# Gate logits in a score tile, the gate's exp behind the scores' exps, and a reordered start, in a fused attention and mixture-of-experts kernel

## The chip, the cores and the metric

The kernel runs on one core of one Trainium2 chip. The metric is device microseconds of one execution; the median of several runs is compared. A core has five engines that each work through their own list of instructions in order and wait for each other by semaphores: TensorE (PE; its weight loads are shown apart as PEld), VectorE (DVE), ScalarE (ACT), GpSimd (POOL) and SyncE (SP). Transfers are issued from the lists of POOL, SP and ACT and run on 16 DMA engines that the core's queues share.

## The reference

Sliding-window causal attention for 8 batches, 8 heads, 576 positions and head width 64, then a mixture of experts in which each batch as a whole goes to one expert:

```
scores = scale * q @ k.T                      # masked to 0 <= i - j < 64
attn   = softmax(scores);  x = attn @ v       # [B, S, H*D] = [8, 576, 512]
logits = x.mean(axis=1) @ w_gate              # [B, 8]
e      = argmax(logits, axis=1)
gate_w = softmax(logits)[e]
out[b] = gate_w[b] * (relu(x[b] @ w1[e]) @ w2[e])    # w1: 512 x 1024, w2: 1024 x 512
```

All inputs and the output are float32.

## The kernel before, in words

The work is cut into 16 units (`NU`), two for each batch (four heads each). For a unit the kernel loads q and k as bf16 (`load_qk`), transposes them on TensorE (`transpose_qk`: 18 transposes each, then one copy to SBUF, `leave_qk`; q's copy is ACT's, k's mostly VectorE's), computes the scores in three chunks (`scores`: 14 matmuls, one exp on ACT and, except for units 0 and 1, one mask product on VectorE), the products with v (`values`, twice 20 matmuls into `op`, then a reciprocal and a product on VectorE that give `x`), and the transposes of x (`transpose_x`: 10 transposes, two copies on ACT that also sum, and VectorE's `gate_parts`). v is loaded once for a batch (`load_v`, a DMA on SP's queue that is started behind a small write on POOL) and cast into two f16 layouts `va` and `vb` (`cast_part`: "whole" fills va, "low" and "high" fill the two halves of vb, from va on VectorE or from the f32 tile on POOL).

When both units of a batch are through, `gate(b)` multiplies the parts by ones (tile `gl`, 8 columns), and VectorE takes the largest logit (`gmx`, MAX8), its index (`graw`, FIND_INDEX8), the clamped index (`eidx`) and the bias (`gnm`); POOL loads the index into a register and issues the loads of the chosen expert's w1 and w2. `gate_weight(b)` is the gate's own exp on ACT (`gex`) and a reciprocal on VectorE (`gatew`). The expert's work comes in 13 chunks for a batch: eight up products (`expert_up`: 8 matmuls into `php`, relu on ACT into `hT`) and five down products (`expert_down`, numbered mt = 0, 1, 2, 4, 3; 8 or 16 matmuls into `pso`, a copy `ob` on VectorE, a DMA to the output).

The order on each engine is the order in which the program is written: nothing reorders it. A start part is written out by hand up to unit 3. Then a loop over t = 4 .. 19 works on unit t and calls `experts(pace)` between its pieces; each call puts out expert chunks, from a stream of all batches, until their summed weight reaches the pace. The gate of batch t/2 - 1 stands inside step t when t is even, between the second and the third chunk of scores (for t = 4 between the first and the second). `busy(n)` puts out n matmuls of a constant on TensorE, whose result nobody reads.

All PSUM tiles (scores, `op`, transposes, `gl`, `php`, `pso`, the constants' products) come from one pool of four buffers of 128 x 2 x 512 float32 that are handed out in turn (two banks each): a new tile waits until the last reader of the tile four places before it is done. A score tile uses columns 0 to 383 of each of its two halves.

At the end `row_check` (three VectorE operations over all row sums) and `row_flag` make a flag; if it fails, a general version runs. It does not run here.

Of the kernel before, what the change touches and what calls it, by code (L numbers as in the profile page):

```python
# [9 lines left out]
FP32 = mybir.dt.float32  # L10
# [146 lines left out]
def kernel(  # L157
# [22 lines left out]
    def P(ins):  # L180
        tc.keep_in_program_order(ins)
        return ins
# [169 lines left out]
            copy_on(eng, dst.rearrange("p (x r t) -> p x r t", x=2, t=NT), view)  # L352
            kt_tiles[u] = dst

    sp_ps = {}

    def add_outside(u, c):

        sp = psum.tile([128, 2, 512], FP32, tag="ps", name="sp")
# [4 lines left out]
        sp_ps[u, c] = sp  # L364

    def scores(u, c):
        qT, kT = qt_tiles[u], kt_tiles[u]
        masked = (u, c) in sp_ps
        if not masked:
            sp_ps[u, c] = psum.tile([128, 2, 512], FP32, tag="ps", name="sp")  # L370
        sp = sp_ps[u, c]

        def mm(s, half, kblk, qblk, n):
            P(nc.tensor.matmul(  # L374
                out=sp[64 * half:64 * half + 64, s,
                       64 * (qblk - 6 * c):64 * (qblk - 6 * c) + n],
                lhsT=kT[64 * s:64 * s + 64, ts(kblk, 64)],
                rhs=qT[64 * s:64 * s + 64, 64 * qblk:64 * qblk + n],
                start=not masked, stop=not masked or kblk >= g0 + 4,
                tile_position=(64 * s, 64 * half)))  # L380
# [8 lines left out]
        P(nc.scalar.activation(out=pt, in_=sp[:, :, 0:384], func=AF.Exp, scale=scale))  # L389
        if not masked:  # L390
            P(nc.vector.tensor_tensor(  # L391
                out=pt, in0=pt, in1=masks[:, c].rearrange("p s g w -> p s (g w)"),
                op=ALU.mult))
        pt_tiles[u, c] = pt
# [88 lines left out]

    gate_in = {}

    def gate(b, both=True):
        gl = psum.tile([128, 2, 512], FP32, tag="ps")
        P(nc.tensor.matmul(out=gl[:, 0, 0:E], lhsT=onesf, rhs=gparts[b],
                           start=True, stop=True))
        glog = gl[:, 0, 0:E]  # L490
        gmx = small.tile([128, 8], FP32, tag="gmx")
        P(nc.vector.max(out=gmx, in_=glog))
        graw = small.tile([128, 8], U32, tag="graw")
        P(nc.vector.max_index(out=graw, in_max=gmx, in_values=glog))
# [3 lines left out]
        P(nc.vector.tensor_scalar(out=gnm, in0=gmx[:, 0:1], scalar1=-1.0 / S,  # L498
                                  scalar2=None, op0=ALU.mult))
        gate_in[b] = gl, gnm  # L500
        if both:
            gate_weight(b)

        ereg = nc.gpsimd.alloc_register(f"er{b}")
        P(nc.gpsimd.load(ereg, eidx[0:1, b, 0:1]))
        experts_of[b] = ds(nc.gpsimd.snap(ereg, donate=True), 1)
        weights[b] = (wpool.tile([128, KB, F], FP16, tag="w1t", name=f"w1t{b}"),
                      wpool.tile([128, FB, Dm], FP16, tag="w2t", name=f"w2t{b}"))

    def gate_weight(b):  # L510
        gl, gnm = gate_in[b]
        glog = gl[:, 0, 0:E]
        gex = small.tile([128, E], FP32, tag="gex")
        gsum = small.tile([128, 1], FP32, tag="gsum")
        P(nc.scalar.activation(out=gex, in_=glog, func=AF.Exp, bias=gnm,
                               scale=1.0 / S, accum_out=gsum))
        P(nc.vector.reciprocal(out=gatew[:, b:b + 1], in_=gsum))  # L517
# [48 lines left out]
    def expert_down(b, mt):  # L566
        w2t, hT = weights[b][1], h_tiles[b]
        pso = psum.tile([128, 2, 512], FP32, tag="ps")
        ob = opool.tile([128, Dm], FP32, tag="ob")
        if mt < 4:  # L570
            for fb in range(FB):
                P(nc.tensor.matmul(  # L572
                    out=pso[:, 0, :], lhsT=hT[:, fb, ts(mt, 128)],
                    rhs=w2t[:, fb, :], start=(fb == 0), stop=(fb == FB - 1)))
            P(nc.vector.tensor_copy(out=ob, in_=pso[:, 0, :]))  # L575
            P(nc.sync.dma_start(out=out[b, ts(mt, 128), :], in_=ob))
        else:

            for fb in range(FB):
                for hf in range(2):  # L580
                    P(nc.tensor.matmul(  # L581
                        out=pso[64 * hf:64 * hf + 64, 0, 0:256],
                        lhsT=hT[:, fb, 512:576],
                        rhs=w2t[:, fb, ts(hf, 256)],
                        start=(fb == 0), stop=(fb == FB - 1),
                        tile_position=(0, 64 * hf)))
            P(nc.vector.tensor_copy(out=ob[:, 0:256], in_=pso[:, 0, 0:256]))
# [30 lines left out]
    def expert_chunks():  # L618
        for b in range(B):
            for ft in range(FB):  # L620
                yield (lambda b=b, ft=ft: expert_up(b, ft)), 1.0
            for mt in (0, 1, 2, 4, 3):
                yield (lambda b=b, mt=mt: expert_down(b, mt)), (1.7 if mt < 4 else 0.9)

    stream = expert_chunks()
    acc = [0.0]

    def experts(amount):

        acc[0] += amount  # L630
        while acc[0] > 0.0:
# [3 lines left out]
            nxt[0]()  # L635
            acc[0] -= nxt[1]

    per_step = (8 * 1.0 + 4 * 1.7 + 0.9) / 2
    START = 3

    def busy(n):

        sp = psum.tile([128, 2, 512], FP32, tag="ps", name="idle")
        for _ in range(n):
            P(nc.tensor.matmul(out=sp[:, 0, :], lhsT=spin[:, 0:128], rhs=spin,
                               start=True, stop=True))


    pool0 = {}
# [35 lines left out]
    for c in range(3):  # L685
        scores(0, c)
    make_masks()
    transpose_qk(1, 0)
    transpose_qk(1, 1)
    cast_part(0, "high", nc.gpsimd)  # L690
    cast_part(0, "low", nc.gpsimd)
    load_qk(3)
    load_qk(4)
    cast_part(0, "whole")
    cast_v(1)
    for c in range(3):
        add_outside(1, c)
    for c in range(3):
# [25 lines left out]
    transpose_x(1, eng=V, parts=False)  # L724
    transpose_qk(3, 0)
# [15 lines left out]
    experts(1.0)  # L741
    transpose_x(2)
    values(3, 1)
    experts(1.0)
    transpose_qk(4, 0)
    transpose_qk(4, 1)
    experts(1.0)
    transpose_x(3)

    for t in range(START + 1, NU + LAG):  # L750
        pace = per_step / 8.0 * 0.96
        on, prev, ahead = t < NU, START + 1 < t <= NU, t + 1 < NU

        def next_gate():
            b = t // 2 - 1
            gate(b)
# [92 lines left out]
```

## Time and profile before

| | |
|---|---|
| runs of before | 233.86, 234.08, 235.32 us; median 234.08 |
| profiled execution | 234.69 us, of which the profile's span is 233.0 us |
| TensorE busy / granted clock | 205.6 us (88%) / 0.981 |
| VectorE, ACT, POOL busy | 140.1 us (60%), 122.5 us (53%), 41.2 us (18%) |
| DMA | 45.64 MB, 196 GB/s on average |
| first expert product / last expert product ends | 33.06 us / 225.8 us |

A row of the page or of the timeline gives the start and the length of an instruction or a group in us, the engine, the line of the kernel, the operation, the tile written and those read, and the shape. What stands in brackets is the time that the engine was idle just before, and what ended that idle time. In a view by windows the columns are the stretch, its length, busy time and (in brackets) number of instructions of an engine, the clock granted to TensorE as a share of full speed, the share of the DMA engines' time, and GB/s. In the chain of waits each row is a piece of the work that ended last: start, length, engine, tile, line.

### The profile page before, as it was taken

Reading aid. Unit: us, or ns where it says so; the run is one execution under the profiler, and the core shown is the slowest. Engines: PE = TensorE matmul, PEld = TensorE weight load, DVE = VectorE, ACT = ScalarE, POOL = GpSimd, SP = SyncE. Lnnn points to the kernel's source line nnn. Section 1 sums busy time; section 2 is a strip of 40 time slices with the busy share of each in tenths; the row PEclk is TensorE's granted clock in tenths of the full one; section 3 lists DMA queues with packets and bytes.
Section 4 is the critical chain, followed back from the end, with each engine's and each line's share of the span. In section 5 each row is a group of like instructions: output and inputs, shape, how many; then the busy total and the mean of one; then the engine's idle time right before and its main releaser. Section 6 shows DMA issues by size and latency. Waiting matters only on the chain.

```text
span 233.0 us, 6978 instructions
## 1 busy us (share of the span) xinstructions
PE 205.6 (88%) x3012; PEld 142.2 (61%) x3012; DVE 140.1 (60%) x314; ACT 122.5 (53%) x206; POOL 41.2 (18%) x69
## 2 busy tenths in 40 slices
PE   7656889999799899989999899999998999979970
PEld 2335767745587557855686457856686568639630
DVE  2639596578757777478656777467766672440140
ACT  2344686851668338670957356853677247406300
POOL 7146260055000330025000700020002000200000
PEclk9999599999999999999999999999999999999998
DMA  5999899999999999989999799989911993299231
GB/s 62 242 255 234 134 183 219 246 248 224 230 236 262 263 201 245 231 242 173 238 228 299 132 226 234 251 211 220 258 56 11 204 240 114 26 225 245 89 130 67
DMA packets 29910, 45.64 MB, mean 196 GB/s; under 512 B 2480, under 2 KB 21936, under 8 KB 29872
## 3 DMA queue, kind: packets, MB, share of 16 engines
q0 software_dynamic: 13840, 26.22, 62.8%
q1 hardware_dynamic: 15232, 18.88, 26.9%
q8 instruction: 25, 0.41, 0.7%
q10 hardware_dynamic: 800, 0.03, 0.2%
q14 instruction: 13, 0.11, 0.1%
HBM read 61.90 MB, written 9.44 MB: 306 GB/s over the span
## 4 chain that ended last, share of the span: by engine, by line
PE 50%; DMA 17%; ACT 14%; DVE 13%; issue 3%; POOL 1%; POOLq 0%; ACTq 0%
PE php L558 22%; DMA w1t<-in_moe_w_dram 13%; PE pso L572 13%; ACT xT L458 4%; DMA kn<-in_k_dram 4%; ACT pt L389 4%; PE tp L334 4%; PE op L413 4%; ACT hT L562 3%; PE tp L450 3%; DVE x L429 2%; DVE pt L391 2%; PE sp L374 2%; PE pso L581 2%; DVE dst L303 2%
## 5 line engine op out<-in xcount | busy, mean ns | idle before, releaser
L558 PE MATMUL php<-xT,w1t 128*128 128x288 f16 x512 | 71.6, 288 | 3.3 <-DMA w1t<-in_moe_w_dram 2.2
L562 ACT ACTIVATE hT<-php,gatew 128x576 f16<-128x576 f32 x64 | 47.5, 747 | 32.0 <-PE php L558 31.5
L572 PE MATMUL pso<-w2t,hT 128*128 128x512 f16 x256 | 60.2, 380 | 1.9 <-DVE ob L575 0.8
L558 PEld LDWEIGHTS <-w1t 128*128 128x128 f16 x512 | 54.6, 115 | 10.4 <-DMA w1t<-in_moe_w_dram 3.0
L389 ACT ACTIVATE pt<-sp 128x768 f16<-128x768 f32 x48 | 37.7, 814 | 10.0 <-PE sp L374 10.0
L572 PEld LDWEIGHTS <-hT 128*128 128x128 f16 x256 | 23.1, 98 | 27.6 <-issue 2.4
L575 DVE COPY ob<-pso 128x512 f32<-128x512 f32 x32 | 22.0, 688 | 23.5 <-PE pso L572 23.4
L458 ACT ACTIVATE xT<-tp 128x576 f16<-128x576 f16 x28 | 17.9, 647 | 32.6 <-PE tp L450 32.6
L535 POOL DMA_DIRECT2D w1t<-in_moe_w_dram x7 | 5.0, 717 | 143.8 <-DVE gatew L517 102.7
L391 DVE TENSOR_TENSOR pt<-pt,masks 128x768 f16<-128x768 f16 x42 | 23.3, 555 | 9.8 <-ACT pt L389 9.1
L429 DVE TENSOR_TENSOR x<-op,linv 128x640 f16<-128x640 f32 x32 | 26.4, 825 | 1.1
L303 DVE COPY dst<-tp 128x1152 bf16<-128x1152 bf16 x14 | 19.0, 1356 | 8.7 <-PE tp L334 8.6
L347 ACT COPY dst<-tp 128x1152 bf16<-128x1152 bf16 x16 | 17.9, 1122 | 9.0 <-PE tp L334 9.0
L413 PE MATMUL op<-vb,pt 128*64 128x65 f16 x320 | 16.8, 196 | 4.5 <-DVE pt L391 1.4
L413 PEld LDWEIGHTS <-pt 128*64 128x64 f16 x640 | 13.5, 110 | 11.0 <-issue 6.2
L374 PE MATMUL sp<-dst 64*64 64x128 bf16 (+1 forms) x672 | 16.0, 219 | 2.8 <-DVE dst L303 1.1
L374 PEld LDWEIGHTS <-dst 64*64 64x64 bf16 x672 | 10.9, 110 | 9.8 <-issue 5.0
L413 PE MATMUL op<-va,pt 128*64 128x65 f16 x320 | 16.5, 197 | 0.0
L480 DVE SCALAR_TENSOR_TENSOR gpart<-wg,pooled,gpart 128x8 f32<-128x8 f32 x21 | 4.8, 227 | 18.5 <-ACT xT L458 18.4
L303 DVE COPY vb<-va 64x1152 f16<-64x1152 f16 (+1 forms) x30 | 13.9, 464 | 0.6
L450 PE MATMUL tp<-identh,x 128*128 128x128 f16 x160 | 12.6, 231 | 1.5 <-DVE x L429 1.1
L450 PEld LDWEIGHTS <-x 128*128 128x128 f16 x160 | 10.7, 104 | 4.2 <-DVE x L429 2.9
(70 smaller groups left out, 165.5 us busy)
## 6 DMA issues: line engine op xcount, KB each, us to landing
w2t<-in_moe_w_dram POOLq DMA_DIRECT2D x8, 1024.0 KB, 16.4
out_dram<-ob SPq DMA_DIRECT2D x32, 256.0 KB, 8.1
w1t<-in_moe_w_dram POOLq DMA_DIRECT2D x7, 1024.0 KB, 8.9
qn<-in_q_dram POOLq DMA_DIRECT2D x16, 288.0 KB, 12.8
kn<-in_k_dram POOLq DMA_DIRECT2D x16, 288.0 KB, 14.5
w1t<-in_moe_w_dram POOLq DMA_DIRECT2D x2, 512.0 KB, 6.4
out_dram<-ob SPq DMA_DIRECT2D x16, 64.0 KB, 6.9
vn<-in_v_dram SPq DMA_DIRECT2D x8, 0.2 KB, 19.5
```

What stands on the lines that cost most here:

```text
L303: P(eng.tensor_copy(out=out, in_=in_))
L374: P(nc.tensor.matmul(out=sp[64 * half:64 * half + 64, s, 64 * (qblk - 6 * c):64 * (qblk - 6 * c) + n], lhsT=kT[64 * s:64 * s + 64, ts(kblk ...
L389: P(nc.scalar.activation(out=pt, in_=sp[:, :, 0:384], func=AF.Exp, scale=scale))
L391: P(nc.vector.tensor_tensor(out=pt, in0=pt, in1=masks[:, c].rearrange("p s g w -> p s (g w)"), op=ALU.mult))
L413: P(nc.tensor.matmul(out=op[64 * half:64 * half + 64, xx, 65 * jj:65 * jj + 65], lhsT=pt[:, s, 64 * (g % 6):64 * (g % 6) + 64], rhs=win, s ...
L429: P(nc.vector.tensor_tensor(out=x[:, :, h0 * D:(h0 + 2) * D].rearrange("p j (x c) -> p x j c", x=2), in0=view[:, :, :, 0:64], in1=li[:, :, ...
L450: P(nc.tensor.transpose(out=tp[:, kl, ts(jj, 128)], in_=x[:, jj, x_chunk(b, kb)], identity=identh))
L458: P(nc.scalar.activation(out=xT[:, kb, :], in_=tp[:, kl, 0:S], func=AF.Copy, accum_out=pooled[:, b, kb:kb + 1]))
L558: P(nc.tensor.matmul(out=php[:, sc, 0:288], lhsT=w1t[:, kb, cols], rhs=xT[:, kb, ts(sc, 288)], start=(kb == 0), stop=(kb == KB - 1)))
L562: P(nc.scalar.activation(out=hT[:, ft].rearrange("p (sc s) -> p sc s", sc=2), in_=php[:, :, 0:288], func=AF.Relu, scale=gatew[:, b:b + 1]))
L572: P(nc.tensor.matmul(out=pso[:, 0, :], lhsT=hT[:, fb, ts(mt, 128)], rhs=w2t[:, fb, :], start=(fb == 0), stop=(fb == FB - 1)))
L575: P(nc.vector.tensor_copy(out=ob, in_=pso[:, 0, :]))
```

## The change

- `gate(b)` takes a home tile: the logits go into columns 384 to 391 of a score tile of the current unit, which is allocated early by the new `score_tile`; for t = 4 that of chunk 1, for later even t that of chunk 2, for gate 0 that of unit 2's chunk 1. Gate 7 has no scores beside it and keeps a tile of its own.
- `gate_weight(b)`, the gate's exp, is put behind the scores' exp of that chunk (behind all three for gate 0).
- k's copy out of PSUM (`leave_qk`) in the loop goes to ACT when the last expert chunk put out was a down product, to VectorE when it was an up product. The copy of down product mt = 1 goes to ACT.
- The start: unit 0's casts of v move from POOL to VectorE and the vb casts of unit 1 from VectorE to POOL, behind a small copy `after` that reads vb; key copy of unit 1 to ACT; `load_v(1)` and `load_qk(2)` behind the first exp; `load_v(2)` ahead of gate 0 and `load_v(3)` where that of 2 was; more and narrower `busy` matmuls; q's and k's transposes of unit 4 apart.
- At t = 16 gate 7 comes one `experts` call earlier, with its exp, and `row_check` behind it instead of ahead.

```diff
-    sp_ps = {}
+    sp_ps, on_pe = {}, set()
+
+    def score_tile(u, c):
+        if (u, c) not in sp_ps:
+            sp_ps[u, c] = psum.tile([128, 2, 512], FP32, tag="ps", name="sp")
+        return sp_ps[u, c]
...
     def scores(u, c):
         qT, kT = qt_tiles[u], kt_tiles[u]
-        masked = (u, c) in sp_ps
-        if not masked:
-            sp_ps[u, c] = psum.tile([128, 2, 512], FP32, tag="ps", name="sp")
-        sp = sp_ps[u, c]
+        masked = (u, c) in on_pe
+        sp = score_tile(u, c)
...
-    def gate(b, both=True):
-        gl = psum.tile([128, 2, 512], FP32, tag="ps")
-        P(nc.tensor.matmul(out=gl[:, 0, 0:E], lhsT=onesf, rhs=gparts[b],
+    def gate(b, home=None):
+
+        if home is None:
+            home = psum.tile([128, 2, 512], FP32, tag="ps", name="gl")
+        glog = home[:, 0, 384:384 + E]
+        P(nc.tensor.matmul(out=glog, lhsT=onesf, rhs=gparts[b],
                            start=True, stop=True))
-        glog = gl[:, 0, 0:E]
...
-        gate_in[b] = gl, gnm
-        if both:
-            gate_weight(b)
+        gate_in[b] = glog, gnm
...
-            P(nc.vector.tensor_copy(out=ob, in_=pso[:, 0, :]))
+            copy_on(nc.scalar if mt == 1 else nc.vector, ob, pso[:, 0, :])
...
-                yield (lambda b=b, ft=ft: expert_up(b, ft)), 1.0
+                yield (lambda b=b, ft=ft: expert_up(b, ft)), 1.0, nc.vector
...
-                yield (lambda b=b, mt=mt: expert_down(b, mt)), (1.7 if mt < 4 else 0.9)
+                yield (lambda b=b, mt=mt: expert_down(b, mt)), (1.7 if mt < 4 else 0.9), nc.scalar
...
+            free[0] = nxt[2]
...
-    def busy(n):
+    def busy(n, cols=128):
...
-    busy(13)
+    busy(13, 512)
...
-
-    load_v(1, kt_tiles[0][:, 0:1])
-    load_qk(2)
     for c in range(3):
         scores(0, c)
+
+    load_v(1, pt_tiles[0, 0][:, 0, 0:1])
+    load_qk(2)
     make_masks()
+    busy(10)
     transpose_qk(1, 0)
-    transpose_qk(1, 1)
-    cast_part(0, "high", nc.gpsimd)
-    cast_part(0, "low", nc.gpsimd)
+    transpose_qk(1, 1, leave=False)
+    leave_qk(1, 1, A)
+    cast_v(0)
+
+    after = const.tile([128, 1], FP16)
+    P(nc.gpsimd.tensor_copy(out=after[64:128], in_=vb[0][64:128, 1, 0:1]))
+    cast_part(1, "high", nc.gpsimd)
+    cast_part(1, "low", nc.gpsimd)
     load_qk(3)
     load_qk(4)
-    cast_part(0, "whole")
-    cast_v(1)
+    load_v(2)
+    cast_part(1, "whole")
...
-    busy(1)
+    busy(10)
...
-    busy(1)
+    busy(8)
     pool_mm(1)
     pool_parts()
-    gate(0, False)
+    busy(5)
+    gate(0, score_tile(2, 1))
     load_w1(0)
     load_w2(0)
     load_qk(5)
-    load_v(2, w1_parts()[:, 0, 0, 0:1])
+    load_v(3, w1_parts()[:, 0, 0, 0:1])
     load_qk(6)
-    load_v(3)
     for c in range(3):
         scores(2, c)
-        if c == 0:
-            gate_weight(0)
+    gate_weight(0)
+    busy(8)
...
-    busy(3)
+    busy(12)
...
+    transpose_qk(4, 0)
     experts(1.0)
-    transpose_qk(4, 0)
+    transpose_x(3)
     transpose_qk(4, 1)
     experts(1.0)
-    transpose_x(3)
...
-        if t == NU:
-            okc = row_check()
         if on:
             scores(t, 0)
         experts(pace)
         if t == START + 1:
+            next_gate(score_tile(t, 1))
+        if t == NU:
             next_gate()
+            gate_weight(B - 1)
+            okc = row_check()
...
         if on:
             scores(t, 1)
+        if t == START + 1:
+            gate_weight(t // 2 - 1)
...
-        if START + 1 < t <= NU and t % 2 == 0:
-            next_gate()
+        if START + 1 < t < NU and t % 2 == 0:
+            next_gate(score_tile(t, 2))
         if on:
             scores(t, 2)
+        if START + 1 < t < NU and t % 2 == 0:
+            gate_weight(t // 2 - 1)
...
-            transpose_qk(t + 1, 1)
+            transpose_qk(t + 1, 1, leave=False)
+            leave_qk(t + 1, 1, free[0])
```

More of the change, by code (lines that the diff above doesn't have):

```diff
@@ L353, in leave_qk @@
             kt_tiles[u] = dst
-    sp_ps = {}
+    sp_ps, on_pe = {}, set()
[3 more added lines that the diff above has]
+        return sp_ps[u, c]
     def add_outside(u, c):
-        sp = psum.tile([128, 2, 512], FP32, tag="ps", name="sp")
+        sp = score_tile(u, c)
+        on_pe.add((u, c))
         for s in range(2):
@@ L363, in add_outside @@
                 rhs=outside[:, c].rearrange("p g w -> p (g w)"), start=True, stop=False))
-        sp_ps[u, c] = sp
     def scores(u, c):
         qT, kT = qt_tiles[u], kt_tiles[u]
-        masked = (u, c) in sp_ps
-        if not masked:
-            sp_ps[u, c] = psum.tile([128, 2, 512], FP32, tag="ps", name="sp")
-        sp = sp_ps[u, c]
+        masked = (u, c) in on_pe
+        sp = score_tile(u, c)
         def mm(s, half, kblk, qblk, n):
@@ L510, in gate_weight @@
     def gate_weight(b):
-        gl, gnm = gate_in[b]
-        glog = gl[:, 0, 0:E]
+        glog, gnm = gate_in[b]
         gex = small.tile([128, E], FP32, tag="gex")
@@ L620, in expert_chunks @@
             for ft in range(FB):
-                yield (lambda b=b, ft=ft: expert_up(b, ft)), 1.0
+                yield (lambda b=b, ft=ft: expert_up(b, ft)), 1.0, nc.vector
             for mt in (0, 1, 2, 4, 3):
-                yield (lambda b=b, mt=mt: expert_down(b, mt)), (1.7 if mt < 4 else 0.9)
+                yield (lambda b=b, mt=mt: expert_down(b, mt)), (1.7 if mt < 4 else 0.9), nc.scalar
     stream = expert_chunks()
-    acc = [0.0]
+    acc, free = [0.0], [nc.vector]
     def experts(amount):
@@ L636, in experts @@
             acc[0] -= nxt[1]
+            free[0] = nxt[2]
     per_step = (8 * 1.0 + 4 * 1.7 + 0.9) / 2
     START = 3
-    def busy(n):
+    def busy(n, cols=128):
         sp = psum.tile([128, 2, 512], FP32, tag="ps", name="idle")
         for _ in range(n):
-            P(nc.tensor.matmul(out=sp[:, 0, :], lhsT=spin[:, 0:128], rhs=spin,
-                               start=True, stop=True))
+            P(nc.tensor.matmul(out=sp[:, 0, 0:cols], lhsT=spin[:, 0:128],
+                               rhs=spin[:, 0:cols], start=True, stop=True))
     pool0 = {}
@@ L752, with next_gate @@
         on, prev, ahead = t < NU, START + 1 < t <= NU, t + 1 < NU
-        def next_gate():
+        def next_gate(home=None):
             b = t // 2 - 1
-            gate(b)
+            gate(b, home)
             load_w1(b)
```

## The prediction

> **What bounds the kernel now.** First the page: busy shares and the granted clock.
>
> ```profile
> PE 205.6 (88%) x3012; PEld 142.2 (61%) x3012; DVE 140.1 (60%) x314; ACT 122.5 (53%) x206; POOL 41.2 (18%) x69
> ...
> PEclk9999599999999999999999999999999999999998
> ```
>
> TensorE is busy for 88% of the span, no other engine for more than 60%. From about 33 us to the last product the kernel is a TensorE stream with gaps; ahead of that it is a start-up chain with one stretch at half clock (the 5). So I ask of each edit whether it closes a TensorE gap or opens one. The second view is the timeline around a gate, here batch 3 (t = 8); the number behind each start is a duration, the bracket the idle time before it and what ended it.
>
> ```profile
> 99.82 0.28 PE L488 MATMUL gl<-gpart,onesf 128*128 128x8 f32 x2
> ...
> 100.06 0.36 PE L374 MATMUL sp<-dst 64*64 64x64 bf16 x14
> ...
> 100.75 0.56 DVE L391 TENSOR_TENSOR pt<-pt,masks 128x768 f16<-128x768 f16 x1 [0.31 <-ACT pt L389]
> 100.77 1.89 PE L572 MATMUL pso<-w2t,hT 128*128 128x512 f16 x8 [0.34 <-ACT pt L389]
> 101.34 0.46 DVE L303 COPY vb<-va 64x1152 f16<-64x1152 f16 x1
> 101.83 0.17 DVE L492 MAX8 gmx<-gl 128x8 f32<-128x8 f32 x1
> ...
> 102.11 0.17 DVE L494 FIND_INDEX8 graw<-gmx,gl 128x8 uint32<-128x8 f32 x1
> ...
> 102.57 0.27 ACT L515 ACTIVATE gex<-gl,gnm 128x8 f32<-128x8 f32 x1 [1.23 <-DVE gnm L498]
> ...
> 102.83 0.80 ACT L389 ACTIVATE pt<-sp 128x768 f16<-128x768 f32 x1
> ...
> 104.28 0.22 PE L413 MATMUL op<-vb,pt 128*64 128x65 f16 x1 [0.78 <-DVE pt L391]
> ```
>
> TensorE finishes the logits at 100.1 and goes straight into the scores of chunk 2 (100.06 in the pipelined starts). VectorE comes to the logits only at 101.83, behind a mask product (it had to wait for ACT) and a copy of v. ACT stands 1.23 us for the gate's bias, and the second products lose 0.34 and 0.78 us to the late exps. That is what the change goes for.
>
> **The change part by part.** *Logits in the home tile.* The program of the changed kernel, read engine by engine with its waits, has the same TensorE order around the gates, but the first scores matmul of the home tile now waits for VectorE's FIND_INDEX8 (graw), the last reader of the logits in that tile; the tile's exp carries the same wait. TensorE runs in order, so the scores and everything behind them stand: down products, transposes, first products of the next chunk. In batch 3 the scores can start at 102.11 + 0.17 + 0.05 = 102.33 instead of 100.06, a new wait of 2.27 us (0.05 from a release to the start: POOL's casts, quoted below, end at 18.25 and the product that waits for them starts at 18.30). VectorE does not get there earlier: its list ahead of MAX8 is unchanged, and it hangs on ACT's exp of chunk 1, whose list ahead is unchanged too. The first and the last of the five gates of this kind (batches 2 to 6):
>
> ```profile
> 75.83 0.36 PE L374 MATMUL sp<-dst 64*64 64x64 bf16 x14
> ...
> 77.61 1.89 PE L572 MATMUL pso<-w2t,hT 128*128 128x512 f16 x8 [0.80 <-DVE ob L575]
> ...
> 77.75 0.17 DVE L494 FIND_INDEX8 graw<-gmx,gl 128x8 uint32<-128x8 f32 x1
> ...
> 174.92 0.36 PE L374 MATMUL sp<-dst 64*64 64x64 bf16 x14
> ...
> 176.92 0.17 DVE L494 FIND_INDEX8 graw<-gmx,gl 128x8 uint32<-128x8 f32 x1
> ...
> 177.79 1.14 PE L558 MATMUL php<-xT,w1t 128*128 128x288 f16 x8 [0.45 <-ACT gex L515]
> ```
>
> New starts: 77.97 against 75.83, and 177.14 against 174.92. What this costs is read where the old stream would have stood anyway. The chain gives the lengths of the pieces, without overlap:
>
> ```profile
> 104.59 1.83 PE pso L572 x8
> 106.42 0.62 PE tp L334 x18
> ...
> 110.86 0.29 PE sp L374 x12
> ...
> 113.44 1.10 PE php L558 x8
> ```
>
> Batch 3: 102.33 + 0.29 + 1.83 + 0.62 = 105.07 for the first second-product, which today starts at 104.28: +0.8 (its exp and mask are ready by about 104.1, so the two old gaps are swallowed, not added). Batch 2: 77.97 + 0.29 + 0.62 = 78.88 against 77.61: +1.3. Batch 6: 177.14 + 0.29 + 1.10 + 0.62 = 179.15 against 177.79: +1.4. Batch 4 has batch 3's order (+0.8), batch 5 has batch 6's (+1.4). Sum 5.7. The exp itself moves little: from 102.83 to about 102.7, since its scores come late. So the tile that is saved and the place ahead of the gate's exp bring what is already netted here, and no more.
>
> The Trainium skill, "PSUM — Partial Sum Buffer", section "PSUM bank collisions raise a hardware error", says that a matmul writing and VectorE reading the same bank and quadrant must be kept apart by a semaphore even at different columns. No run shown here has them in one bank; by that rule this wait cannot be dropped for the columns being free, and the sum stays as above, whereas without the wait it would be that of the first rival.
>
> *Keys and one down product to ACT, and the other gaps.* In the second-product half of each batch VectorE loses a key copy and one result copy; ACT (53% busy) takes them behind the gate's exp, where its next work waits for TensorE. Cost nothing; if that cover were gone, the next scores would wait at most the key copy's length. What it frees:
>
> ```profile
> 46.72 0.39 PE L488 MATMUL gl<-gpart,onesf 128*128 128x8 f32 x2 [0.40 <-DVE gpart L480]
> ...
> 52.28 0.22 PE L413 MATMUL op<-vb,pt 128*64 128x65 f16 x1 [0.30 <-DVE vb L303]
> ...
> 52.94 0.19 PE L413 MATMUL op<-vb,pt 128*64 128x65 f16 x1 [0.43 <-DVE vb L303]
> ...
> 60.39 0.36 PE L374 MATMUL sp<-dst 64*64 64x64 bf16 x14 [0.65 <-DVE ob L587]
> ...
> 61.62 1.17 PE L558 MATMUL php<-xT,w1t 128*128 128x288 f16 x8 [0.86 <-DMA w1t<-in_moe_w_dram]
> ...
> 84.36 0.73 PE L450 MATMUL tp<-identh,x 128*128 128x128 f16 x10 [0.48 <-DVE x L429]
> ...
> 184.30 0.73 PE L450 MATMUL tp<-identh,x 128*128 128x128 f16 x10 [0.30 <-DVE x L429]
> ```
>
> The x transposes wait for VectorE three times (0.48, 0.30, 0.30: first and last shown); all three should go: -1.1. At t = 4 and 5, 0.30 + 0.43 + 0.65 go with the relief (-1.4). The 0.86 for batch 1's w1 should go too, because the third v is out of its way: -0.9. Against that stands gate 1 itself: key transposes now end one up product ahead of the scores, so those wait for the key copy (about 0.4), and the home tile's wait comes to about 0.7 after the 0.40 above is gone: between 0 and +1.4, I take +0.7. Together -1.1 - 1.4 - 0.9 + 0.7 = -2.7.
>
> *The start.* Casts of batch 0's v swap engines, v 1 goes behind the first exp, v 2 ahead of gate 0, filler matmuls are added.
>
> ```profile
> 15.36 2.89 POOL L303 CAST vb<-vn 64x1088 f16<-64x1088 f32 x2 [2.90 <-DMA vn<-in_v_dram]
> ...
> 18.30 0.19 PE L413 MATMUL op<-vb,pt 128*64 128x65 f16 x1 [0.95 <-POOL vb L303]
> ...
> 24.46 0.19 DVE L668 TENSOR_TENSOR prod<-wg,pool 128x32 f32<-128x32 f32 x1 [0.38 <-PE pool L660]
> ...
> 27.05 2.29 PE L450 MATMUL tp<-identh,x 128*128 128x128 f16 x20 [0.34 <-ACT pt L389]
> ...
> 27.54 1.51 POOL L532 DMA_DIRECT2D w1t<-in_moe_w_dram  x2 [6.37 <-issue]
> ...
> 32.42 0.71 PE L374 MATMUL sp<-dst 64*64 64x64 bf16 x42 [1.03 <-ACT dst L301]
> ...
> 32.91 0.44 POOL L226 CAST vn<-w1t 128x1 f32<-128x1 f16 x1 [1.71 <-DMA w1t<-in_moe_w_dram]
> ```
>
> The first second-product loses its 0.95 us behind POOL; POOL's 2.89 us now serve the other half and end near 20.2, so gate 0 comes between 0 and 1.2 us earlier; I take 1.0 (w1 issued at 26.5). The x transposes then wait for three exps (0.8 each) and the gate's exp instead of one exp: start about 27.5 instead of 27.05, but at full clock 2 x 0.73 instead of 2.29. Scores of t = 3 come near 31.8, 0.6 earlier. But the up products also need w1's first half: issue to landing was 32.9 - 27.5 = 5.4 us with the queues nearly empty; now v 2 (1.18 MB) and four q/k loads, issued some 2 us later than now behind POOL's casts, are under way with it. Ends: 5.4 us (landing 31.9) and twice that (37.3). I take 6.5, nearer the short end since v 2 is shared only in part: 33.0, against 32.9 now. Start: 0, between -1.0 and +2.5 (most of the halved case; later products hide none of it).
>
> What the fillers are for is seen in the windows (TensorE's busy time, clock):
>
> ```profile
> 19.42:22.84 3.42, 2.04 (x72) 1.00 1.16 214
> 22.84:26.25 3.41, 2.67 (x59) 0.50 1.21 204
> ```
>
> A window with 60% busy was followed by one at half clock. The Trainium skill, "TensorE: Matmul & The Clock Gate", section "HAM oscillation — how this bites in real kernels", asks only that no idle gap be over about 3.4 us; this trace differs, since 1.4 us idle in all was enough. By that rule the fillers buy nothing and the start would be some 0.8 us worse than I have it.
>
> *The tail.* Gate 7 keeps its own tile. Its logits come one up product earlier in TensorE's order and the row check goes behind it.
>
> ```profile
> 197.97 0.39 PE L488 MATMUL gl<-gpart,onesf 128*128 128x8 f32 x2
> ...
> 209.77 8.03 PE L558 MATMUL php<-xT,w1t 128*128 128x288 f16 x64 [1.20 <-DMA w1t<-in_moe_w_dram]
> ```
>
> The logits cannot start before 197.97 (their operand), so TensorE stands about 0.9 us one up product earlier; w1 comes some 0.7 earlier and its wait of 1.20 shrinks by what TensorE lost. Between -0.7 and +0.5; I take 0.
>
> **Sum.** +5.7 - 2.7 + 0 + 0 = +3.0. The profiled execution took 234.69 us (span 233.0 and 1.7 around it), so 237.7 by it; the median of the runs, 234.08, lies 0.6 below it: 237.1.
>
> **The rivals.** *The wait costs nothing* (other side, faster): VectorE takes up the gate at once when the logits are there, so that MAX8 and FIND_INDEX8 end 0.5 us after them and not 2.2. It decides at the gates of batches 2 to 6; from a wait under about 1.0 us each gate gains. 5 x 1.7 = 8.5 us less: 228.6. For it: VectorE is only 60% busy and relieved. Against it: the 0.31 it idles before the mask product shows that it waits for ACT there, not for its own backlog. *The start goes wrong*: v 2 delays w1, or TensorE falls to half clock once more while it waits for the gate's exp; +2: 239.1. For it: 1.18 MB of v and four q/k loads of 288 KB, 2.3 MB, ahead of or beside w1. *The start and the gaps give more*: start -1.0, gate 1 at 0 instead of +0.7: 235.4. For it: the lower ends above. *The change does nothing it says*: every move is covered, 234.1.
>
> **How the numbers follow.** Forecast 0.45 (236 to 238.4; a fifth of it under 1%), gate wait free 0.14, start wrong 0.16, more gaps closed 0.23, nothing 0.02. One per cent (2.3 us) is about what a measurement of this kernel can tell from no change. Slower by over 1%: 0.36 + 0.16 = 0.52; within: 0.09 + 0.23 + 0.02 = 0.34; faster: 0.14. The range, 233.6 to 240.0, takes in all but the first rival and the ends of the start's bounds.
>
> **What would show it.** In the profile after: scores matmuls with 2 us of idle time released by VectorE's graw at five gates; no waits for ACT's gex, the x product or batch 1's w1; the home tile's exp hardly earlier; the clock without its half-speed stretch near 25 us; the first up product near 33. If the idle time before those scores is under 1 us, the forecast is wrong at its main term; if the first up product is later than 34.5, at the start.

## The result, and the profile after

The changed kernel takes 252.78 us (median of four runs, 251.78 to 254.73) against 234.37 us (four runs, 233.86 to 235.32): 1.079 times the time, 95% interval 1.071 to 1.087. The prediction had the sign and missed the size by a wide margin: 18.4 us were lost, where it had 3.0, and its range ended at 240.0. Ratios and intervals leave out runs more than 1.5% above the fastest run of the same kernel, and where a kernel below has such runs its median is given without them.

The page of the changed kernel, the two parts that were shown of the kernel before:

```profile
PE 214.1 (86%) x3060; PEld 146.8 (59%) x3060; DVE 125.8 (50%) x299; ACT 136.0 (54%) x221; POOL 40.5 (16%) x70
...
PEclk9979965999999979999999799979999899999997
```

The copies have moved as intended (VectorE 140.1 to 125.8 us, ACT 122.5 to 136.0). But TensorE is busy 8.5 us longer. More filler matmuls are 1.9 of that (8.9 us of them now, 7.0 before); the same 512 up products take 75.7 us instead of 71.6, and the 256 wide down products 62.2 instead of 60.2. The clock row says why: before, it had one dip, a 5 near 25 us; now there are six, two at the start (the stretch near 25 us is gone, but there are others at 15.5 to 18.9 and 32.6 to 42.8 us) and four spread over the loop. The mean granted clock is 0.940 against 0.981.

Who TensorE waited for in the changed kernel (us in total, times, longest):

```profile
PE sp L377 <- DVE graw L499: 11.7, 7, 2.2
PE php L560 <- DMA w1t<-in_moe_w_dram: 5.6, 1, 5.6
PE sp L377 <- DVE dst L303: 2.0, 2, 1.3
...
PE tp L453 <- DVE x L432: 1.1, 2, 0.7
...
PE op L416 <- DVE vb L303: 0.8, 2, 0.4
```

Two waits lead, one of 11.7 us in seven pieces and one of 5.6 us in one. The same place as in the prediction, the gate of batch 3, in the timeline of the changed kernel:

```profile
109.88 0.28 PE L494 MATMUL sp<-gpart,onesf 128*128 128x8 f32 x2
...
110.80 0.56 DVE L394 TENSOR_TENSOR pt<-pt,masks 128x768 f16<-128x768 f16 x1 [0.30 <-ACT pt L392]
111.38 0.46 DVE L303 COPY vb<-va 64x1152 f16<-64x1152 f16 x1
111.86 0.17 DVE L497 MAX8 gmx<-sp 128x8 f32<-128x8 f32 x1
...
112.15 0.17 DVE L499 FIND_INDEX8 graw<-gmx,sp 128x8 uint32<-128x8 f32 x1
...
112.37 0.36 PE L377 MATMUL sp<-dst 64*64 64x64 bf16 x14 [2.20 <-DVE graw L499]
...
113.50 0.26 ACT L517 ACTIVATE gex<-sp,gnm 128x8 f32<-128x8 f32 x1
```

VectorE comes to the logits as late as before, behind the mask product that hangs on ACT; the scores stand for 2.20 us behind FIND_INDEX8. ACT no longer waits for the bias. What follows is not the same at all gates. Windows of the changed kernel around this gate and around the next one (stretch, length, busy time and count of PE, PEld, DVE, ACT, POOL, then clock, DMA share, GB/s):

```profile
107.69:111.10 3.41, 2.48 (x32) 2.08 (x31) 2.25 (x6) 3.41 (x8) 0.00 (x0) 1.00 1.10 316
111.10:114.51 3.41, 2.14 (x24) 0.94 (x23) 2.00 (x9) 1.36 (x4) 0.93 (x2) 1.00 0.10 36
134.99:138.41 3.42, 1.46 (x24) 1.33 (x21) 2.97 (x8) 2.70 (x5) 0.00 (x0) 1.00 1.07 342
138.41:141.82 3.41, 3.16 (x36) 1.86 (x36) 1.05 (x6) 2.18 (x4) 1.95 (x3) 0.50 0.36 54
141.82:145.23 3.41, 3.41 (x37) 1.52 (x37) 1.64 (x3) 0.02 (x1) 2.37 (x5) 1.00 0.93 162
```

The clock changes only at borders 3.41 us apart. At batch 3 a border (111.10) cuts the stall in two, both windows keep 2.1 us or more of busy time, and the clock holds. At batch 4 the stall lies in one window, which has 1.46 us (43%) of busy time, and the next 3.41 us run at half clock. So at batches 2, 5 and 6 too: at four of these five gates the stall is paid a second time.

The start, in the timeline of the changed kernel, and the windows from there on (the second fence):

```profile
27.11 1.50 POOL L534 DMA_DIRECT2D w1t<-in_moe_w_dram  x2 [3.79 <-DVE pt L394]
...
31.21 0.71 PE L377 MATMUL sp<-dst 64*64 64x64 bf16 x42 [1.21 <-ACT dst L301]
37.48 4.03 PE L560 MATMUL php<-xT,w1t 128*128 128x288 f16 x16 [5.56 <-DMA w1t<-in_moe_w_dram]
```

```profile
29.18:32.59 3.41, 1.52 (x54) 1.21 (x53) 3.27 (x6) 2.88 (x4) 1.57 (x3) 1.00 1.12 237
32.59:36.01 3.42, 0.00 (x0) 0.00 (x0) 1.78 (x4) 1.31 (x2) 0.00 (x0) 0.50 1.22 219
36.01:39.42 3.41, 1.95 (x9) 1.21 (x10) 0.00 (x0) 0.00 (x0) 1.51 (x3) 0.50 1.22 213
39.42:42.83 3.41, 3.41 (x32) 2.05 (x31) 0.55 (x2) 1.48 (x2) 0.11 (x1) 0.50 1.07 220
```

w1 is issued at 27.11, earlier than before (27.54), but the first up product, which needs its first half, starts at 37.48 instead of 33.06, 10.4 us behind the issue. TensorE is idle for 5.56 us ahead of it (31.92 to 37.48). The clock falls at 32.59, behind a window with 1.52 us of busy time that holds only the first 0.7 us of this wait, and it stays at half until 42.83, so the first 16 up products take 4.03 us.

Set side by side, the first up product of each batch is later than before by 4.4 (batch 0), 7.6, 10.1, 10.9, 12.8, 15.8, 18.1 and 17.9 us (batch 7). The loss is made at the start and at the gates; of the five gates with a stall of over 2 us the one behind which the clock did not fall has the smallest step (0.9, from batch 2 to 3). The tail adds nothing.

### The profile page after: what moved, and what is told of

It reads as the page before. It is cut to its first block, busy times and chain, and to the rows that moved or that the text cites. A ratio compares the mean times of both kernels' runs of the same rounds, so it can differ in the third digit from the quotient of the medians.

```text
span 250.3 us, 7091 instructions
## 1 busy us (share of the span) xinstructions
PE 214.1 (86%) x3060; PEld 146.8 (59%) x3060; DVE 125.8 (50%) x299; ACT 136.0 (54%) x221; POOL 40.5 (16%) x70
## 4 chain that ended last, share of the span: by engine, by line
PE 64%; ACT 13%; DVE 9%; DMA 8%; issue 2%; POOL 1%; POOLq 0%
PE php L560 23%; PE pso L574 22%; PE tp L334 6%; ACT xT L461 5%; PE op L416 5%; ACT pt L392 5%; DMA kn<-in_k_dram 4%; DMA w1t<-in_moe_w_dram 4%; ACT hT L564 3%; PE sp L377 3%; PE pso L583 2%; PE tp L453 2%; DVE vb L303 2%; DVE x L432 2%; DVE pt L394 1%
## 5 line engine op out<-in xcount | busy, mean ns | idle before, releaser
L560 PE MATMUL php<-xT,w1t 128*128 128x288 f16 x512 | 75.7, 299 | 5.8 <-DMA w1t<-in_moe_w_dram 5.6
L560 PEld LDWEIGHTS <-w1t 128*128 128x128 f16 x512 | 55.5, 117 | 15.5 <-DMA w1t<-in_moe_w_dram 6.1
L574 PE MATMUL pso<-w2t,hT 128*128 128x512 f16 x256 | 62.2, 389 | 0.3 <-ACT pt L392 0.3
L392 ACT ACTIVATE pt<-sp 128x768 f16<-128x768 f32 x48 | 37.7, 815 | 18.9 <-PE sp L377 18.9
L303 DVE COPY ob<-pso 128x512 f32<-128x512 f32 x24 | 16.6, 690 | 31.7 <-PE pso L574 31.6
L377 PE MATMUL sp<-dst 64*64 64x128 bf16 (+1 forms) x672 | 16.4, 223 | 14.9 <-DVE graw L499 11.7
L461 ACT ACTIVATE xT<-tp 128x576 f16<-128x576 f16 x28 | 17.9, 647 | 12.4 <-PE tp L453 12.4
L377 PEld LDWEIGHTS <-dst 64*64 64x64 bf16 x672 | 11.7, 111 | 21.8 <-issue 16.5
L347 ACT COPY dst<-tp 128x1152 bf16<-128x1152 bf16 x16 | 18.0, 1126 | 9.3 <-PE tp L334 9.0
L430 DVE RECIPROCAL linv<-op 128x10 f32<-128x10 f32 x32 | 7.0, 218 | 27.5 <-PE op L416 27.5
L301 ACT COPY dst<-tp 128x1152 bf16<-128x1152 bf16 x9 | 10.1, 1126 | 10.4 <-PE tp L334 10.2
L303 DVE CAST va<-vn 128x1152 f16<-128x1152 f32 x16 | 12.2, 765 | 4.9 <-DMA vn<-in_v_dram 4.8
## 6 DMA issues: line engine op xcount, KB each, us to landing
vn<-in_v_dram SPq DMA_DIRECT2D x8, 0.2 KB, 17.9
```

The source lines that it names most:

```text
L303: P(eng.tensor_copy(out=out, in_=in_))
L347: P(nc.scalar.copy(out=dst.rearrange("p (x r t) -> p x r t", x=2, t=NT), in_=view))
L377: P(nc.tensor.matmul(out=sp[64 * half:64 * half + 64, s, 64 * (qblk - 6 * c):64 * (qblk - 6 * c) + n], lhsT=kT[64 * s:64 * s + 64, ts(kblk ...
L461: P(nc.scalar.activation(out=xT[:, kb, :], in_=tp[:, kl, 0:S], func=AF.Copy, accum_out=pooled[:, b, kb:kb + 1]))
L560: P(nc.tensor.matmul(out=php[:, sc, 0:288], lhsT=w1t[:, kb, cols], rhs=xT[:, kb, ts(sc, 288)], start=(kb == 0), stop=(kb == KB - 1)))
L574: P(nc.tensor.matmul(out=pso[:, 0, :], lhsT=hT[:, fb, ts(mt, 128)], rhs=w2t[:, fb, :], start=(fb == 0), stop=(fb == FB - 1)))
```

## The experiments

The theory after the result: the gates' waits are as forecast, and the half clock behind them and v 2 beside w1 make the rest. Rivals: the copies on ACT, the exp's new place or the rest of the start make part of it; or the shared tile costs in another way than by TensorE's idle time. The kernels were run in three groups, each beside the kernel before on the same chip: the first four below (before: 234.32 us), the one with nine fillers and the three of "What the rest gains" (234.26), and the others (233.98). Each ratio is to the kernel before of its group.

**All logits in tiles of their own**, the rest of the change kept (a line for each of the three calls):

```diff
-    gate(0, score_tile(2, 1))
+    gate(0)
-            next_gate(score_tile(t, 1))
+            next_gate()
-            next_gate(score_tile(t, 2))
+            next_gate()
```

> The changed kernel with one part undone: the logits of every gate go to a PSUM tile of their own again; all else as changed. Theory (two sources: the scores' wait for VectorE's index at seven gates, with the half-clock stretch that follows it, worth 11 to 12 us, and v 2 ahead of the first w1, worth about 7 us): 240 to 242 us, no half-clock stretch after the gates of batches 2 to 6, first up product still near 37.5 us. Rival (the half-clock stretches come from the new fillers and copies, the wait costs only its 5.7 us net): 246 to 248 us, stretches stay.

Measured: 236.86 us (seven runs), ratio 1.010 (1.006 to 1.013): below the range expected, so 15.9 us of the 18.4 hang on the shared tile, more than any forecast of mine gave it. In the profiled run the clock stays at full speed at the gates. The start is as bad as in the changed kernel, in a timeline row of this kernel:

```profile
38.57 4.03 PE L560 MATMUL php<-xT,w1t 128*128 128x288 f16 x16 [6.16 <-DMA w1t<-in_moe_w_dram]
```

**v 2 and v 3 loaded where the kernel before loads them**, the rest of the change kept:

```diff
-    load_v(2)
     cast_part(1, "whole")
...
-    load_v(3, w1_parts()[:, 0, 0, 0:1])
+    load_v(2, w1_parts()[:, 0, 0, 0:1])
     load_qk(6)
+    load_v(3)
```

> The changed kernel with the loads of v 2 and v 3 put back to where they stood (v 2 behind the first half of w1, v 3 behind q/k 6); all else as changed. Theory: w1's first half lands at about 32 us instead of 37.4, first up product at 32.5 to 33, no half-clock stretch from 32.6 on, 245 to 246 us. Rival (w1 is late because POOL issues it behind its longer casts and the q/k loads): first up product after 35 us, 250 us or more.

Measured: 243.03 us (two runs, 241.5 and 244.56), ratio 1.036 (1.027 to 1.045). By these v's place is worth 9.8 us; with the two longer runs (246.54 and 247.83) the median is 245.55 and it is worth 7.2, so the price is known only roughly. In this kernel w1's two halves land 5.7 and 7.4 us behind their issue; in the changed kernel 10.3 and 12.0. First the row of this kernel's view of the w1 tile, then its first up product:

```profile
DMA to landing us min/median/max: 5.7/6.5/7.4
```

```profile
34.04 3.45 PE L560 MATMUL php<-xT,w1t 128*128 128x288 f16 x16 [0.90 <-DMA w1t<-in_moe_w_dram]
```

The same row of the changed kernel:

```profile
DMA to landing us min/median/max: 10.3/11.2/12.0
```

3.4 us of it are the later first product of the changed kernel. The rest fits the clock, but was not measured apart: in the profiled run (247.83 us) the half clock at batch 0 lasts from 34.7 to 38.1 us instead of from 32.6 to 42.8, and there are three drops at the gates of batches 2 to 6 instead of four. The rival falls (the product comes before 35 us), but the theory holds only in part: the product comes 1 us later than expected, and the half clock behind 32.6 us is shorter, not gone. The mean clock differs from run to run: 0.983, 0.961, 0.967 and 0.952, in the order of the times above.

**Both undone**, that is the two diffs above together.

> Both undone, the rest of the change kept (gate's exp behind the scores' exps, keys and one down product on ACT, casts of v swapped, fillers, gate 7 earlier). Theory: 229 to 233 us, faster than before by the gaps that went (some 5 us less what the later w1 takes). Rival (the rest of the change costs too): 236 us or more.

Measured: 231.27 us, ratio 0.984 (0.978 to 0.991): faster than the kernel before. So everything else in the change together gains about 3 us, and shared tile and v 2 make the whole loss. With only one of them in, the tile costs 11.8 us (231.27 to 243.03; 14.3 with the two longer runs) and v's place 5.6 us (231.27 to 236.86).

**The shared tile alone**, put into the kernel before, for gates 1 to 6, with the exp behind the scores:

```diff
+        if home is None:
+            home = psum.tile([128, 2, 512], FP32, tag="ps", name="gl")
+        glog = home[:, 0, 384:384 + E]
...
+            gate(b, t == NU, home)
...
+            next_gate(score_tile(t, 1))
...
+            next_gate(score_tile(t, 2) if on else None)
         if on:
             scores(t, 2)
+        if START + 1 < t < NU and t % 2 == 0:
+            gate_weight(t // 2 - 1)
```

> The kernel before with one part of the change alone: logits of the gates 1 to 6 in the score tile, the gate's exp behind that chunk's exp. Theory: the wait alone brings the half-clock stretches, about 1.6 us each, beside its own 5.7 to 6.4 us: 242 to 246 us. Rival (no half clock without the rest of the change): 240 to 241 us and a granted clock above 0.975.

Measured: 246.78 us, ratio 1.051 (1.043 to 1.058). The start is the old one and the loss is there, a little more than expected. Windows of this kernel at the gate of batch 3, which drops, and of batch 2, which a border at 78.79 cuts, and which does not:

```profile
102.68:106.09 3.41, 1.34 (x19) 0.73 (x19) 1.94 (x9) 2.02 (x5) 0.12 (x1) 1.00 0.73 245
106.09:109.51 3.42, 3.42 (x43) 2.02 (x42) 1.40 (x4) 0.80 (x3) 3.42 (x6) 0.50 0.63 74
```

```profile
75.37:78.79 3.42, 2.16 (x24) 1.26 (x17) 3.03 (x7) 2.04 (x4) 0.00 (x0) 1.00 1.14 275
78.79:82.20 3.41, 2.60 (x40) 1.46 (x39) 1.58 (x8) 2.07 (x4) 1.34 (x2) 1.00 1.05 258
```

**The same with TensorE kept busy in the stall**: nine matmuls of a constant between the logits and the scores that wait, at the gates of batches 2 to 6. The scores start no earlier; only the idle time goes.

```diff
+        if fill:
+            spare = psum.tile([128, 2, 512], FP32, tag="ps", name="idle")
+            for _ in range(9):
+                P(nc.tensor.matmul(out=spare[:, 0, :], lhsT=spin[:, 0:128], rhs=spin,
+                                   start=True, stop=True))
```

> The kernel before with the home tile alone, and with nine matmuls of a constant (128x512, into a tile of their own) between the logits and the scores that wait for graw, at the gates of batches 2 to 6. Theory (the idle TensorE ahead of graw, 2.1 us inside one window of 3.41 us, brings the next window to half clock): the scores still wait for VectorE, and the products begin as late as with the home tile alone, but TensorE is busy for most of the wait, so the clock stays at full speed behind the gates and the time falls from 246.8 us to between 239 and 242. Rival (the extra comes of something else that the wait shifts, a late DMA or VectorE falling behind): no change, 245 to 248 us.

Measured: 240.21 us, ratio 1.027 (1.022 to 1.033). The theory holds and the rival falls: work that nobody reads makes the kernel 6.6 us faster. Timeline and windows of this kernel at the gate of batch 3:

```profile
102.15 0.28 PE L494 MATMUL sp<-gpart,onesf 128*128 128x8 f32 x2
102.39 2.10 PE L508 MATMUL idle<-spin 128*128 128x512 bf16 x9
104.64 0.36 PE L377 MATMUL sp<-dst 64*64 64x64 bf16 x14
```

```profile
102.36:105.77 3.41, 3.26 (x28) 1.51 (x28) 2.07 (x9) 2.02 (x4) 0.00 (x0) 1.00 0.86 275
105.77:109.19 3.42, 3.42 (x50) 1.89 (x49) 2.37 (x5) 1.46 (x4) 3.34 (x6) 1.00 0.62 77
```

From the logits to the scores it is 2.49 us, with the tile alone 2.48 (102.27 to 104.75), so the stall itself is the same; the window behind runs at full clock. The one drop of this profile in the loop (47.75 to 51.16) is at the gate of batch 1, which shares a tile too and has no fillers. The fillers' own tile also shifts the rotation of the four PSUM buffers; that this has a part in the gain was not tried.

**Four of these matmuls instead of nine** (`range(4)`).

> As the kernel with nine constant matmuls ahead of the waiting scores, but with four: about 0.9 us busy and 1.2 us idle at each gate. The clock view is to tell how much idle time in one window of 3.41 us is borne. Theory (the window's busy share decides, and the kernel before bore gaps of up to 0.9 us at these places): clock held, 240 us, like nine. Rival (any gap over 1 us brings the half clock): 245 to 247 us.

Measured: 240.43 us, ratio 1.028 (1.026 to 1.031), the same as with nine. The waits and a window of this kernel:

```profile
PE sp L377 <- DVE graw L499: 7.1, 6, 1.2
```

```profile
101.36:104.77 3.41, 2.19 (x23) 1.02 (x23) 1.97 (x8) 2.02 (x4) 0.02 (x1) 1.00 0.79 257
104.77:108.19 3.42, 3.42 (x51) 1.83 (x49) 2.37 (x5) 1.36 (x3) 3.42 (x6) 1.00 0.61 80
```

1.2 us of idle time in a window (64% busy) are borne.

**What the rest gains.** Three kernels: the copies on ACT alone, put into the kernel before; the gate's exp behind the scores' exps alone, logits in their own tile; and both, with the earlier gate 7.

```diff
-            P(nc.vector.tensor_copy(out=ob, in_=pso[:, 0, :]))
+            copy_on(nc.scalar if mt == 1 else nc.vector, ob, pso[:, 0, :])
...
-            transpose_qk(t + 1, 1)
+            transpose_qk(t + 1, 1, leave=False)
+            leave_qk(t + 1, 1, free[0])
```

> The kernel before with the key copies and the copy of the down product mt = 1 on ACT beside down products, and nothing else. Theory (VectorE's backlog makes the gaps ahead of the x transposes and the scores): 232 to 233.3 us, and those gaps are gone. Rival (ACT is as late as VectorE was: the gate's bias still holds it): 234.3 us.

Measured: 233.77 us, ratio 0.997 (0.994 to 1.000): 0.5 us, if anything. The waits of this kernel for w1, for VectorE's x and for ACT's gex:

```profile
PE php L558 <- DMA w1t<-in_moe_w_dram: 3.1, 3, 1.8
...
PE tp L450 <- DVE x L429: 0.5, 1, 0.5
PE pso L572 <- ACT gex L515: 0.5, 1, 0.5
PE php L558 <- ACT gex L515: 0.5, 1, 0.5
```

Two of the three waits for x are gone, as the prediction said, and so is the wait of 0.65 us for VectorE's ob at t = 5. But the waits for the gate's exp stand, and the time hardly moves. In part w1 takes the gain: batch 1's first up product starts at 61.75, behind a wait of 1.80 us for w1, where it started at 61.62 behind 0.86.

```diff
         def next_gate():
             b = t // 2 - 1
-            gate(b)
+            gate(b, t == NU)
...
         if on:
             scores(t, 2)
+        if START + 1 < t < NU and t % 2 == 0:
+            gate_weight(t // 2 - 1)
```

> The kernel before with the gate's exp behind the scores' exps of its step, the logits in their own tile, and nothing else. Theory (ACT's 1.2 us wait for the gate's bias delays the exp of the scores and so the second products by 0.3 to 0.8 us at each gate): 231.5 to 233 us, with no idle time of TensorE put down to gex. Rival (VectorE's mask product is late anyway): 234.3 us.

Measured: 231.15 us, ratio 0.987 (0.984 to 0.990). The best part of the change is this move, 3.1 us. The gate of batch 3 in this kernel:

```profile
101.55 1.89 PE L572 MATMUL pso<-w2t,hT 128*128 128x512 f16 x8 [0.34 <-ACT pt L389]
...
101.98 0.86 ACT L389 ACTIVATE pt<-sp 128x768 f16<-128x768 f32 x1
...
103.25 0.55 DVE L391 TENSOR_TENSOR pt<-pt,masks 128x768 f16<-128x768 f16 x1
103.36 0.27 ACT L515 ACTIVATE gex<-gl,gnm 128x8 f32<-128x8 f32 x1 [0.53 <-DVE gnm L498]
103.37 0.69 PE L334 MATMUL tp<-ident,qn 128*64 128x128 bf16 x18
```

The exp of chunk 2 now follows 1.13 us behind the logits' scores (100.85 to 101.98; before, 100.06 to 102.83), and no second product waits for it.

> The start of the kernel before; in the loop the change's copies on ACT, the gate's exp behind the scores' exps and the earlier gate 7, with the logits in a tile of their own. Theory (the gain of the change comes all from the loop: the term that the prediction called the relief of VectorE, -2.7, and the tail 0): 230 to 232 us, as with both undone (231.3). Rival (the reordered start has a part of that gain): 233 us or more.

Measured: 231.17 us (five runs), ratio 0.985 (0.980 to 0.990), the same as with v and tile undone (231.27) and as the exp alone (231.15). So beside the exp's new place the copies on ACT, the rest of the reordered start and the earlier gate 7 give nothing that can be measured.

**The gate earlier.** If the tile costs only because VectorE comes late, logits that come ahead of the scores of chunk 1 should share a tile for nothing:

```diff
         if t == START + 1:
             next_gate()
+        if START + 1 < t < NU and t % 2 == 0:
+            next_gate(score_tile(t, 2))
...
         if on:
             scores(t, 1)
```

> The kernel before with the gate's exp behind the scores' exps and, at the gates of batches 2 to 6, the logits in the tile of the scores of chunk 2, but issued ahead of the scores of chunk 1; gates 1 and 7 in tiles of their own. Theory (the home tile costs only because VectorE reaches the logits 2 us late, behind the mask product that hangs on ACT): VectorE takes the gate up ahead of that mask product, graw is done before the scores of chunk 2 are due, no wait for graw and no half clock behind the gates; the logits wait up to 0.5 us for their operand: 230 to 233.5 us. Rival (sharing the tile costs by itself, wherever the gate stands): 238 us or more.

Measured: 231.78 us, ratio 0.990 (0.987 to 0.992). The gate of batch 3 in this kernel:

```profile
98.32 0.39 PE L493 MATMUL sp<-gpart,onesf 128*128 128x8 f32 x2 [0.40 <-DVE gpart L483]
...
99.60 0.17 DVE L498 FIND_INDEX8 graw<-gmx,sp 128x8 uint32<-128x8 f32 x1
...
100.03 0.36 PE L377 MATMUL sp<-dst 64*64 64x64 bf16 x14
```

FIND_INDEX8 ends at 99.77 and the scores of chunk 2 start at 100.03 without a wait. The tile itself costs nothing; its price was the order. With the same place and tiles of their own:

> The same with all logits in tiles of their own. Theory: the same within 1 us, the tile that is saved is worth nothing; w1 and w2 are issued some 3 us earlier than now, so the wait of up to 1 us for w1 at the first up products goes: 229.5 to 232.5 us. Rival (the tile is worth something): over 1 us slower than with the home tile at the same place.

Measured: 231.91 us, ratio 0.991 (0.989 to 0.994). The same: the tile that is saved is worth nothing either. The waits for w1 did not go (1.9 us in two pieces, with the exp's move alone 2.6 in three), and the earlier w1 gains nothing over that move.

## Why the prediction was wrong

**Right:** the sign; the bound (a TensorE stream, in which a new gap behind the gates costs); and the gate wait, its largest term. The waits were forecast as 2.14 (batch 2), 2.27 (batch 3) and 2.22 us (batch 6) and measured 2.07, 2.20 and 2.13. Its net price is seen undisturbed where the fillers hold the clock. There the logits of batches 2 to 7 start later than before by an amount that grows from batch to batch by 0.80, 0.86, 0.97, 1.36 and 1.34 us, 5.3 in all; the sum had 1.3, 0.8, 0.8, 1.4 and 1.4, 5.7 in all. The first and the last of the six, in that kernel (before: 75.61 and 197.97):

```profile
77.14 0.28 PE L494 MATMUL sp<-gpart,onesf 128*128 128x8 f32 x2
...
204.83 0.39 PE L494 MATMUL gl<-gpart,onesf 128*128 128x8 f32 x2
```

Right too: the tail at 0, no waits for gex left, and that the rival in which VectorE takes up the gate at once falls, by the argument that it was given.

**The step that failed:** "What this costs is read where the old stream would have stood anyway". The sum priced each stall by the time that the stream stands and left the clock out. At four of five gates, in the changed kernel and in the one with the tile alone, the stall also halved the clock for the next 3.41 us; with TensorE busy all that time, that is up to 1.7 us a drop. The kernel with the tile alone has four such drops and loses 6.6 us against its twin with fillers, which has none there: 1.6 to 1.7 a drop. The prediction had the row for it: it showed that a window with 60% busy time was followed by half clock at the start, and drew the conclusion for the fillers alone, not for the five stalls of over 2 us that it had itself just put in. The Trainium skill, "TensorE: Matmul & The Clock Gate", section "HAM oscillation — how this bites in real kernels", asks for no idle gap over about 3.4 us; by that rule the stalls would be harmless, and the runs here differ: 2.2 us were enough.

**The second step, mis-sized:** the start, taken as 0. Its bounds for w1's first half were 5.4 us and twice that (landing 31.9 to 37.3); 6.5 was chosen "since v 2 is shared only in part", and 10.3 was measured, the other end; w1 was issued at 27.11 and not at 26.5. The bound on the time, +2.5, was too small as well: the first product alone moved by 4.4, and it begins at half clock. Moving v 2 back is worth 5.6 us without the shared tile and 7.2 to 9.8 with it. The rival "v 2 delays w1" named the mechanism, at a price of 2.

**The third, mis-sized:** the relief, -2.7. The copies on ACT are worth 0.5 us by the medians, with an interval that reaches no change, not the 2.5 of closed gaps that the sum gave for x and t = 4 and 5. Of these, two x gaps and the 0.65 at t = 5 did close there, but the wait for batch 1's w1 grew by 0.94, and the two gaps at t = 4 stand (0.31 and 0.43): they wait for VectorE's vb. In the changed kernel they stand too (0.8 together, in the waits above), its waits for x are 1.1 us as before, in two pieces, and the key copy ahead of gate 1 costs the scores 1.27 us where the sum had about 0.4. The exp's new place, of which the prediction said that it brings "what is already netted here, and no more", is worth 3.1 us by itself; beside the shared tile that gain was swallowed by the wait, as the netting had it. The wait for batch 1's w1 went, but not for the reason given: it is gone as well with v 2 and v 3 back in their old places (there w1 is waited for once, at batch 0). With the loop's changes behind the start of before it is back (1.96 us); which part of the new start removes it stays open.

Put together from the runs (medians, us): shared tile with the exp behind, clock held, +6.0 (240.21 - 234.26); the clock behind those gates +6.6 (246.78 - 240.21); the v loads +5.6; the copies -0.5; the rest of start and tail 0. That is 17.7, and 18.4 was measured. With the price that the v loads have beside the shared tile, 7.2 to 9.8, it would be 19.3 to 21.9: that price comes from the kernel that scatters most.

## What to carry to other kernels

A stall put into a TensorE stream was priced twice here: by the time that the stream stood, and by the half-speed window that could follow; ask of each new wait of 2 us how much of a 3.4 us window it leaves idle, and if the wait must be, fill it. Before letting a small result share a PSUM tile with the next large one, look where its reader stands in its own engine's list: the writer will wait for that place, and moving the small result ahead of what holds the reader made the sharing free here, while a tile of its own cost nothing either. And when a large transfer is moved ahead of one that a chain waits for, reckon with the slow end of the bounds: it was the one that came here.

## What the runs showed of the hardware that was not expected

- In each profile the clock changes only at borders that lie whole multiples of 3.41 us apart, whatever the kernel does in between. At the gates of batches 2 to 6, windows with 1.2 to 1.5 us of busy time were followed by half clock each time (44% and less: 4 in the changed kernel, 4 with the tile alone, 2 with v 2 moved back), and windows with 2.1 us or more never (2.14 and 2.48 in the changed kernel, 2.16 and 2.60 with the tile alone, 2.19 to 2.26 with four fillers). Between them it is open. With v 2 moved back, these two windows of one profile, of nearly the same busy time, went different ways:

```profile
79.08:82.49 3.41, 1.66 (x10) 0.97 (x8) 3.05 (x7) 1.54 (x3) 0.00 (x0) 1.00 0.74 175
82.49:85.91 3.42, 3.09 (x62) 1.79 (x63) 1.10 (x6) 2.31 (x5) 1.82 (x3) 1.00 0.35 89
...
130.28:133.69 3.41, 1.70 (x26) 1.47 (x25) 2.75 (x7) 2.94 (x6) 0.00 (x0) 1.00 1.10 335
133.69:137.11 3.42, 2.92 (x36) 1.80 (x36) 1.27 (x7) 2.18 (x4) 1.71 (x3) 0.50 0.35 75
```

  The first held wide down products and the logits, the second scores, up products and the logits. At the start the busy time settles even less: in the kernel before, 2.09 us of 102 matmuls held the clock (16.00 to 19.42) and 2.04 us of 72 right behind did not, and with v and tile undone 2.46 us of 57 (21.44 to 24.85) did not either. What counts beside the busy time was not tried.
- The same stall costs a drop or none by where a border falls: with the tile alone a border cuts the one of batch 2, which costs none, and in the changed kernel the one of batch 3. That would explain why the kernel with v 2 moved back scatters more from run to run (241.5 to 247.8 us) than the kernel before (233.3 to 235.6 beside it). It is not shown, since only one run of each kernel has a trace.
- The first 512 KB half of w1 takes 5.2 to 5.7 us from issue to landing without a v load beside it, and 10.3 us beside a v load of 1.18 MB that was issued 3.7 us earlier from SP's queue (11.1 us with all logits in tiles of their own, where the v load was issued 2.8 us earlier): about twice as long.
